# Layer 2's first product by two-by-two blocks: 7 block products in place of 8, cosines on rows of 768 columns, sums of y made on chip

## The chip, the cores and the metric

The program runs on one core of a Trainium2 chip. The metric is the device time of one execution in microseconds (us); lower is better. A core has five engines that run their own instruction streams in order: PE (matmuls; PEld are its weight loads), DVE (vector), ACT (activations), POOL (GpSimd) and SP, which here only issues transfers. Engines wait for each other through semaphores.

## The reference

```python
# attention with random features over 4 sequences of 576 tokens, 8 heads of 64: x is 2304 tokens x 512
phi = lambda x: exp(h - max(h)) / sqrt(m)         # h = x @ omega.T - |x|^2 / 2
x = (phi(q) @ (phi(k).T @ v)) / (phi(q) @ sum(phi(k)) + 1e-6)
# layer 1: 512 -> 1536 -> 512
xn = x / sqrt(mean(x * x) + 1e-6) * rms_g
y = (silu(xn @ w_gate) * (xn @ w_val)) @ w_out
# layer 2: 512 -> 2048 -> 512
h = y @ w_in
out = (h * cos(h)) @ w_out2
```

All is float32. The kernel reaches that accuracy by splitting every operand of a product into a high and a low part of type fp32r and making three products of them (high x high, low x high, high x low), summed in PSUM.

## The kernel before

**Layout.** Activations lie transposed: 128 features on the partitions, tokens along the row. A block is 384 tokens, so 2304 tokens are 6 blocks; two neighbouring blocks are a pair (p = 0, 1, 2). The 512 inputs of a layer are four chunks of 128. A feature block f is 128 columns of the hidden layer: 12 in layer 1, 16 in layer 2.

**Stages.** Attention comes first, with the first four features of layer 1 between its last tiles. Then features 4 to 7 and 8 to 11 of layer 1 run pair by pair, each through `duo` (two features at a time) and `ys` (layer 1's second product). `duo` works on two-by-two blocks: two weight blocks by two halves of the input on one side, two halves of the input by two token blocks on the other, 7 products of combined blocks (names X and Y, by the table `PRODUCTS`) in place of 8; each product is 6 matmuls of 384 columns. Layer 2 follows: for each feature group of `GROUPS2` and each block, one step for each feature: `hidden` makes h in 12 matmuls of 384 columns (4 chunks x 3 parts), ACT and DVE make o = h cos(h) and split it, and `out2` multiplies o by the feature's output weights in 9 matmuls of 512 columns (3 token tiles x 3 parts) into three PSUM banks of sums.

**The cosine.** The chain of one step is: ACT rounds h / 2 pi to an integer (`turns`, L878), DVE subtracts that many turns in two instructions (L879, which reads h in PSUM; L880, which reads two rows in SBUF), ACT takes the sine (L885), DVE multiplies by h (L887, which reads h in PSUM), ACT copies the high part (L888), DVE makes the low part (L890, two rows in SBUF). The step's matmuls of `out2` come two steps after its `hidden`.

**Weights.** The class `Weights` turns the float64 weights into pairs of fp32r, piece by piece (512 columns). A front (DVE L175, L180, L187; ACT L167; POOL L192) makes a float32 piece and keeps it in DRAM. A back reads it again (`b<-kept`) and splits it into a tile of a ring of 20 (ACT L197, POOL L200). For the block products the back also makes sums of pieces (DVE L248, L260, L262, L264). `pace` runs a number of these steps after every unit of the main work, by rates that the main loop sets; `wts.freed` says how many ring tiles are free again.

**Order.** Nothing is scheduled by a program: the order of the code is the order of each engine's queue. `at(d, f)` puts an action off by d units, `unit()` runs what is due.

**Between the layers.** The sums of layer 1's y are completed on DVE (`add_y`, L1118), split (ACT L1070, DVE L1073) and kept in DRAM (`yh_dram`); layer 2 reads blocks of y back (`fetch`, `yhl`). Layer 2's sums over the three feature groups stay in SBUF (`osum`: first group copied, later ones added by `add_up`, L834).

Of the kernel before, what the change touches and what calls it, by code (L numbers as in the profile page):

```python
# [50 lines left out]
FRONT, BACK, BACK_OF_PAIR = 6, 4, 11  # L51
BLOCKED, DONE = "blocked", "done"
# [3 lines left out]
def attention_then_ffn(ctx: ExitStack, tc: tile.TileContext, qT, kT, v, omT, wc1, rms_g, wc2, out, B, H, S, D):  # L56
# [15 lines left out]
    RING, MORE = 20, 2  # L72
# [7 lines left out]
    GROUPS2 = [range(0, 6), range(6, 11), range(11, 16)]  # L80
# [14 lines left out]
    BANKS = {"w": 4, "kv": 2, "q": 2}  # L95
# [3 lines left out]
    def bank(tag, name):  # L99
        return psum.tile([P, 512], F32, tag=tag, name=name, bufs=BANKS[tag])  # L100

# [16 lines left out]
    y_dram = {}  # L118


    class Weights:
# [3 lines left out]
        def __init__(self):  # L125
# [3 lines left out]
            self.todo += [(2, f, e) for f in range(NF2) for e in range(C2)]  # L129
# [10 lines left out]
            self.more = None  # L140
            self.credit = [0.0, 0.0]
            self.first = self.run()
            self.fronts, self.backs = self.all_fronts(), self.all_backs()

        def paired(self, layer, f, e):
            return e if layer == 1 and f not in GROUPS1[0] and e < 2 else None

        def load(self, c, queue=None):
            queue = queue or (nc.scalar if self.early else nc.sync)
            if c < len(self.todo) and c not in self.loaded:  # L150
                self.loaded.add(c)
                layer, f, e = self.todo[c]
# [19 lines left out]
        def front(self, c):  # L172
# [10 lines left out]
            yield  # L183
            self.exponent(c + 1)
# [17 lines left out]
        def split(self, src, key):  # L202
# [5 lines left out]
            if self.paired(layer, f, e) == 0:  # L208
                self.out[1, f, "A11"], self.out[1, f, "A12"] = (t, 0), (t, 256)
# [4 lines left out]
        def ask(self, c):  # L214

            if c in self.kept and c not in self.b:
                b = self.b[c] = conv.tile([P, 512], F32, tag="b", name=f"b{c}", bufs=4)
                nc.sync.dma_start(b, self.kept[c])

        def back(self, c):  # L220
            layer, f, e = self.todo[c]
            whole, one, two = slice(0, 512), slice(0, 256), slice(256, 512)
            while c not in self.kept:
# [32 lines left out]
            self.out[1, f, "S1"], self.out[1, f, "A22"] = (t, 0), (t, 256)  # L256
# [22 lines left out]
            self.out[1, f, "S2"], self.out[1, f, "S3"] = (t, 0), (t, 256)  # L279
            yield  # L280
            self.low(g[:, two], four, at)
            self.out[1, f, "S4"] = (four, 256 * (f % 2))
# [43 lines left out]
        def widen(self, pool):  # L326

            self.more, self.since = pool, self.made

        def buffer(self):  # L330
            c = self.made
            self.made += 1
            more = self.more is not None and (c - self.since) % (RING + MORE) >= RING
            return (self.more if more else wpool).tile([P, 2, 512], F32R, tag="w", name=f"w{c}")

        def room(self):
            wide = self.more is not None and self.made >= self.since + RING
            return self.made < self.freed + RING + (MORE if wide else 0)
# [7 lines left out]
        def pace(self, *rates):  # L346

            for i, rate in enumerate(rates):
# [3 lines left out]
                for _ in range(n):  # L352
                    if next(self.first, DONE) is not DONE:
                        continue
                    if next((self.fronts, self.backs)[i], DONE) in (BLOCKED, DONE):
                        break
                    if i:
                        self.n_back += 1
                    else:
                        self.n_front += 1  # L360
# [159 lines left out]
    with tc.manual_schedule():  # L520
# [59 lines left out]
        def job(n):  # L580
            for _ in range(n):
                if len(combined) < limit[0] and jobs and next(jobs[0], DONE) is DONE:
                    jobs.pop(0)
                    combined.add(len(combined))

        def combinations(p):

            to = t_dram[p] = {n: dram.tile([P, 2, 2, NB], F32, name=f"{n}_dram{p}") for n in ("T1", "T2", "T3", "T4")}
# [25 lines left out]
            for kk in range(2):  # L614
# [31 lines left out]
                lower(s2)  # L646
                keep("T1", kk, s1)
# [20 lines left out]
                lower(s4)  # L668
                keep("T2", kk, s3)
# [4 lines left out]
        def query_step(t, s):  # L674
# [110 lines left out]
        combine = ExitStack()  # L785
# [22 lines left out]
        late = [None]  # L808

        def sum_tile(name):  # L810
            if late[0] is None:
                between.close()
                combine.close()
                late[0] = ctx.enter_context(tc.tile_pool(name="sums", bufs=NBLK, side="right", reuse_waits="tile"))
                wts.widen(ctx.enter_context(tc.tile_pool(name="w2", bufs=MORE, side="right", reuse_waits="tile")))
            return late[0].tile([P, KD * NB], F32, tag="sum", name=name)
# [6 lines left out]
        def put_away(blk, e, ps):  # L823

            y = row(F32, f"y{blk}_{e}") if not more else more[0].tile([P, NB], F32, tag="y", name=f"y{blk}_{e}", bufs=YROWS)
# [6 lines left out]

        def add_up(blk, at, ps):
            nc.vector.tensor_tensor(held[blk][:, at], ps, held[blk][:, at], op=ALU.add)  # L834
# [36 lines left out]
        def hidden(blk, f):  # L871

            w = wts.get(2, f, 0)
            h = bank("w", f"h_ps{blk}_{f}")[:, :NB]
            passes(h, [(two(w, slice(kk * P, (kk + 1) * P)), part(blk, kk)) for kk in range(KD)])
            a, b = row(I32, f"turns{blk}_{f}"), row(F32, f"r{blk}_{f}")

            nc.scalar.activation(a, h, AF.Identity, bias=quarter, scale=1.0 / (2 * math.pi))  # L878
            nc.vector.scalar_tensor_tensor(b, a, -TWO_PI_HI, h, op0=ALU.mult, op1=ALU.add)  # L879
            nc.vector.scalar_tensor_tensor(f32(a), a, -TWO_PI_LO, b, op0=ALU.mult, op1=ALU.add)  # L880
            return h, f32(a)

        def h_cos(blk, f, h, r, front, rate):
            o = fp.tile([P, 2, NB], F32R, tag="t", name=f"o{blk}_{f}", bufs=3)
            nc.scalar.activation(r, r, AF.Sin, bias=half_pi)  # L885
            wts.pace(front / 4, rate / 2)
            nc.vector.tensor_tensor(r, h, r, op=ALU.mult)  # L887
            nc.scalar.copy(o[:, 0], r)  # L888
            wts.pace(front / 4, rate / 2)
            nc.vector.tensor_tensor(o[:, 1], r, f32(o[:, 0]), op=ALU.subtract)  # L890
            return o

        oacc = {}

        def first_sum(blk, j, ps):
            if j == 0:
                held[blk] = sum_tile(f"osum{blk}")
            a = held[blk][:, j * DM:(j + 1) * DM]
            if j % 2:
                nc.vector.tensor_copy(a, ps)  # L900
            else:
                nc.scalar.copy(a, ps)

        def put_out(blk, j):
            t = blk * TPB + j
            nc.sync.dma_start(out[t * P:(t + 1) * P, :], held[blk][:, j * DM:(j + 1) * DM])

        def out2(g, blk, f, o, first, last):
            if first:
# [393 lines left out]
```

## Time and profile before

| | |
|---|---|
| median of 3 runs | 991.6 us (991.59 to 991.62) |
| profiled execution, time | 991.8 us |
| its span in the profile | 990.0 us |
| PE busy | 976.8 us, 99% |
| PEld (weight loads) busy | 923.6 us |
| DVE busy | 674.1 us, 68% |
| ACT busy | 512.1 us, 52% |
| POOL busy | 361.7 us, 37% |
| moved by DMA | 194.58 MB, mean 197 GB/s |
| mean granted clock of PE | 0.996 |

The profile is one execution; its time is its span and 1.8 us around it, and lies 0.2 us above the median. PE has something in flight in 99% of the span, so what is left to read is how fast its matmuls follow each other and where the few idle microseconds are. Matmuls overlap: the pace is the distance between starts, not the duration of one.

### The profile page before, as it was taken

Reading aid. Unit: us, or ns where it says so; the run is one execution under the profiler, and the core shown is the slowest. Engines: PE = TensorE matmul, PEld = TensorE weight load, DVE = VectorE, ACT = ScalarE, POOL = GpSimd, SP = SyncE. Lnnn points to the kernel's source line nnn. Section 1 sums busy time; section 2 is a strip of 40 time slices with the busy share of each in tenths; the row PEclk is TensorE's granted clock in tenths of the full one; section 3 lists DMA queues with packets and bytes.
Section 4 is the critical chain, followed back from the end, with each engine's and each line's share of the span. In section 5 each row is a group of like instructions: output and inputs, shape, how many; then the busy total and the mean of one; then the engine's idle time right before and its main releaser. Section 6 shows DMA issues by size and latency. Waiting matters only on the chain.

```text
span 990.0 us, 16129 instructions
## 1 busy us (share of the span) xinstructions
PE 976.8 (99%) x5905; PEld 923.6 (93%) x5905; DVE 674.1 (68%) x1195; ACT 512.1 (52%) x1117; POOL 361.7 (37%) x333
## 2 busy tenths in 40 slices
PE   9999999998999999999999989999999999999998
PEld 8988999998999999999999988999999999999997
DVE  5786778788854466686665767666667776666565
ACT  7787776675434442536443545554444544344433
POOL 2133348647926865476441742211112310000000
PEclk9999999999999999999999999999999999999999
DMA  8555268876696989657988875433224432014201
GB/s 303 159 170 181 83 227 285 269 286 223 247 326 237 364 291 346 222 164 276 356 291 302 323 253 193 125 131 129 64 107 161 161 143 78 1 37 154 98 32 64
DMA packets 81438, 194.58 MB, mean 197 GB/s; under 512 B 8016, under 2 KB 38864, under 8 KB 81360
## 3 DMA queue, kind: packets, MB, share of 16 engines
q1 hardware_dynamic: 79920, 188.78, 54.8%
q10 hardware_dynamic: 1440, 4.78, 1.4%
q8 instruction: 46, 0.75, 0.3%
q14 instruction: 32, 0.26, 0.1%
HBM read 136.38 MB, written 57.15 MB: 195 GB/s over the span
## 4 chain that ended last, share of the span: by engine, by line
PE 89%; DVE 4%; POOL 2%; DMA 2%; issue 2%; ACT 2%; SPq 0%; ACTq 0%; DVEq 0%; POOLq 0%
PE h_ps L798 20%; PE X L1062 10%; PE y L1141 10%; PE Y L1062 8%; PE gv_ps L798 7%; PE o_ps L792 7%; PE o_ps L791 7%; PE o_ps L790 7%; PE y_ps L863 4%; PE kv_ps L562 4%; PE num_ps L439 2%; PE kp_ps L401 2%; PE qp_ps L401 2%; PE eT_ps L419 1%; DMA x_dram<-xhl 1%
## 5 line engine op out<-in xcount | busy, mean ns | idle before, releaser
L798 PE MATMUL h_ps<-yhl,w 128*128 128x384 f32 x1152 | 217.5, 337 | 0.0
L798 PEld LDWEIGHTS h_ps<-yhl,w 128*128 128x128 f32 x1152 | 205.2, 188 | 8.2
L192 POOL TENSOR_TENSOR f<-f,raw 128x512 f32<-128x512 f32 x68 | 93.9, 1381 | 286.1 <-DVE raw L187 251.9
L200 POOL TENSOR_TENSOR w<-b,w 128x512 fp32r<-128x512 f32 x72 | 95.2, 1327 | 80.6 <-ACT w L197 71.3
L885 ACT ACTIVATE turns<-turns,half_pi 128x384 f32<-128x384 f32 x96 | 59.2, 617 | 109.9 <-DVE turns L880 109.9
L790 PE MATMUL o_ps<-w,o 128*128 128x512 f32 x288 | 112.5, 391 | 2.6 <-ACT o L888 2.6
L792 PE MATMUL o_ps<-w,o 128*128 128x512 f32 x288 | 114.6, 398 | 0.0
L791 PE MATMUL o_ps<-w,o 128*128 128x512 f32 x288 | 114.2, 396 | 0.0
L798 PE MATMUL gv_ps<-xhl,w 128*128 128x384 f32 x576 | 108.3, 336 | 1.1 <-DVE eT L429 0.4
L798 PEld LDWEIGHTS gv_ps<-xhl,w 128*128 128x128 f32 x576 | 100.7, 188 | 2.2 <-DVE eT L429 0.7
L1141 PE MATMUL y<-t,w 128*128 128x384 f32 x576 | 101.0, 334 | 0.0
L1141 PEld LDWEIGHTS y<-t,w 128*128 128x128 f32 x576 | 99.9, 188 | 0.0
L890 DVE TENSOR_TENSOR o<-turns,o 128x384 fp32r<-128x384 f32 x96 | 55.9, 583 | 51.8 <-ACT o L888 51.2
L887 DVE TENSOR_TENSOR turns<-h_ps,turns 128x384 f32<-128x384 f32 x96 | 53.4, 556 | 44.2 <-ACT turns L885 43.4
L888 ACT CAST o<-turns 128x384 fp32r<-128x384 f32 x96 | 49.3, 513 | 65.9 <-DVE turns L887 65.3
L1062 PE MATMUL X<-T,w 128*128 128x384 f32 x432 | 80.7, 334 | 0.0
L879 DVE SCALAR_TENSOR_TENSOR r<-turns,h_ps 128x384 f32<-128x384 int32 x96 | 53.1, 553 | 39.0 <-ACT turns L878 38.9
L1062 PEld LDWEIGHTS X<-T,w 128*128 128x128 f32 x432 | 75.4, 188 | 0.0
L878 ACT ACTIVATE turns<-h_ps,quarter 128x384 int32<-128x384 f32 x96 | 55.5, 579 | 35.2 <-PE h_ps L798 34.9
L792 PEld LDWEIGHTS o_ps<-w,o 128*128 128x128 f32 x288 | 54.3, 189 | 11.9 <-DVE o L890 0.3
L790 PEld LDWEIGHTS o_ps<-w,o 128*128 128x128 f32 x288 | 54.2, 188 | 11.6 <-ACT o L888 3.0
L880 DVE SCALAR_TENSOR_TENSOR turns<-turns,r 128x384 f32<-128x384 int32 x96 | 61.6, 641 | 3.3
(98 smaller groups left out, 1714.5 us busy)
## 6 DMA issues: line engine op xcount, KB each, us to landing
raw<-wc SPq DMA_DIRECT2D x59, 512.0 KB, 5.1
yhl<-yh_dram SPq DMA_DIRECT2D x32, 768.0 KB, 5.7
T<-T_dram SPq DMA_DIRECT2D x20, 768.0 KB, 9.1
kept<-f SPq DMA_DIRECT2D x56, 256.0 KB, 5.3
b<-kept SPq DMA_DIRECT2D x56, 256.0 KB, 4.6
B<-x_dram SPq DMA_DIRECT2D x15, 768.0 KB, 6.6
x_dram<-xhl SPq DMA_DIRECT2D x12, 768.0 KB, 5.8
s<-x_dram SPq DMA_DIRECT2D x24, 384.0 KB, 5.9
```

Source lines behind the costliest of these rows:

```text
L192: nc.gpsimd.tensor_tensor(f32(f), f32(f), rest, op=ALU.add)
L200: nc.gpsimd.tensor_tensor(t[:, 1, to], src, f32(t[:, 0, to]), op=ALU.subtract)
L790: nc.tensor.matmul(o, w[0], x[0], start=first, stop=False)
L791: nc.tensor.matmul(o, w[0], x[1], start=False, stop=False)
L792: nc.tensor.matmul(o, w[1], x[0], start=False, stop=last)
L798: nc.tensor.matmul(o, w[i], x[j], start=n == 0, stop=n == len(terms) - 1)
L878: nc.scalar.activation(a, h, AF.Identity, bias=quarter, scale=1.0 / (2 * math.pi))
L880: nc.vector.scalar_tensor_tensor(f32(a), a, -TWO_PI_LO, b, op0=ALU.mult, op1=ALU.add)
L885: nc.scalar.activation(r, r, AF.Sin, bias=half_pi)
L890: nc.vector.tensor_tensor(o[:, 1], r, f32(o[:, 0]), op=ALU.subtract)
L1062: nc.tensor.matmul(o, w[:, i, c + kk * P:c + (kk + 1) * P], x[:, j, kk], start=begin and n == 0, stop=n == 5, skip_group_check=True)
L1141: nc.tensor.matmul(acc[e], w[:, i, e * P:(e + 1) * P], t[:, j], start=f == fs[0] and i + j == 0, stop=f == fs[-1] and j == 1)
```

## The change

Layer 2's first product now works like layer 1's `duo`. A period is one pair of features (f, f + 1) by one pair of blocks, 24 periods in all; its `hidden(k, i)` is one of 7 products of 6 matmuls, and the 36 matmuls of `out2` of the period before stand in runs of 5 or so between them. Layer 1's last `ys` carries the first period's 7 products between its matmuls. The groups of feature pairs are {0, 1, 2}, {3, 4, 5}, {6, 7}; within a group the pairs of blocks take turns.

The results of the products are copied (ACT) or added (DVE) from PSUM into rows of SBUF, two chains (feature by block) side by side, and `cosine` treats them as one row of 768 columns. The high and low parts are still made for each chain (384 columns). The combinations of y that the products need (T1 to T4) are made on POOL (`mix`), ACT and DVE while y is still in SBUF. The sums of layer 2 are no longer held in SBUF over the groups: a run of periods on one pair of blocks leaves its six sums in DRAM, and the next run adds them (`evict`, `ask_sum`); seven runs evict 42 tiles of 256 KB, of which 24 go to DRAM and come back. At the end of a run the seven inputs of the next (768 KB each) are loaded during one period. The weights of layer 2 need the sums of pieces too: seven half tiles for a feature where there were four. Fronts and backs are kept apart from their loads by `LAG_OF_RAW` and `LAG_OF_KEPT` units.

```diff
-    GROUPS2 = [range(0, 6), range(6, 11), range(11, 16)]
+    GROUPS2 = [[0, 1, 2], [3, 4, 5], [6, 7]]
+    PARTS2 = [6, 5, 6]
...
+            while self.too_new(self.loaded_at, c + 1, LAG_OF_RAW):
+                yield BLOCKED
...
+            while self.too_new(self.asked_at, c, LAG_OF_KEPT):
+                yield BLOCKED
...
+        def mix(p, name, kk):
+            a, b, c, d = (whole[2 * p + side, 2 * i + kk] for side, i in ((0, 0), (1, 0), (1, 1), (0, 1)))
+            o, x, y = {"T1": (a, b, a), "T3": (b, c, b), "T2": (c, c, a), "T4": (d, d, c)}[name]
+            nc.gpsimd.tensor_tensor(o, x, y, op=ALU.subtract)
+            at(2, mix_high, p, name, kk, o)
...
+        def hidden(k, i):
...
+            o = banks2[k, acc]
+            seventh(o, 2, p, f, which, name, i in (0, 1, 3))
+            if i in (0, 2, 3, 6):
+                if i in (2, 6) or (k, i) == (0, 0):
+                    rows2[k + (i > 2), i // 2 % 3] = two_rows(F32, f"h{i}_{k}")
+                a = rows2[k, 1][:, 3 - i] if i in (2, 3) else rows2[k + (i > 2), 0][:, int(i == 0)]
+                nc.scalar.copy(a, o)
+            else:
+                a = rows2[k, int(i > 1)][:, (1, 0, 1)[(1, 4, 5).index(i)]]
+                nc.vector.tensor_tensor(a, o, a, op=ALU.add)
+            if i == 1:
+                cosine(k, rows2.pop((k, 0)), ([(k - 1, 2 * periods[k - 1][3] + 1, 2 * periods[k - 1][2])] if k else [])
+                       + [(k, f, 2 * p)])
...
+            elif i == 5:
+                cosine(k, rows2.pop((k, 1)), [(k, f + 1, 2 * p + 1), (k, f, 2 * p + 1)])
...
+            def reduce():
+                nc.vector.scalar_tensor_tensor(b, a, -TWO_PI_HI, h, op0=ALU.mult, op1=ALU.add)
+                nc.vector.scalar_tensor_tensor(r, a, -TWO_PI_LO, b, op0=ALU.mult, op1=ALU.add)
+
+            def cut(i):
+                o = turned[of[i]] = halves("o%d_%d_%d" % of[i])
+                split(o, r[:, i])
+                at(int(of[i][0] + 1 < NPER), lower, o, r[:, i], nc.vector)
+
+            at(1, nc.scalar.activation, a, h, AF.Identity, quarter, 1.0 / (2 * math.pi))
+            at(2, reduce)
+            at(3, nc.scalar.activation, r, r, AF.Sin, half_pi)
+            at(4, lambda: nc.vector.tensor_tensor(r, h, r, op=ALU.mult))
+            for i in range(len(of)):
+                at(5 + i, cut, i)
...
+            share = [0, 3, 6, 6, 7, 7, 7] if begins_run[k] or k + 1 == NPER else [5, 5, 5, 5, 5, 5, 6]
+            for i in range(7):
+                hidden(k, i)
+                unit()
+                for _ in range(share[i]):
+                    next(o)
+                unit()
```

**DVE, in the middle of layer 2.** Before, a step in the first group of features (feature 7 on block 0; `h_ps` is h in PSUM, `turns` and `r` are rows in SBUF, `o` the split result):

```order
L879 SCALAR_TENSOR_TENSOR r0_7_8511<-turns0_7_8510,h_ps0_7_8497 128x384
L880 SCALAR_TENSOR_TENSOR turns0_7_8510<-turns0_7_8510,r0_7_8511 128x384
L887 TENSOR_TENSOR turns0_7_8510<-h_ps0_7_8497,turns0_7_8510 128x384
L890 TENSOR_TENSOR o0_7_8534<-turns0_7_8510,o0_7_8534 128x384
```

Now, DVE in period 8 (pair of blocks 0, third pair of features; `h6`, `h2` are rows of h in SBUF, `Yh`, `Xh` the products in PSUM, `f57`, `raw57`, `b53` pieces of weights):

```order
L1187 TENSOR_TENSOR h6_7_8066<-Yh_8_8083,h6_7_8066 128x384
L1049 TENSOR_TENSOR o7_3_1_8097<-turns7_3_1_7_2_1_8048,o7_3_1_8097 128x384
L190 TENSOR_SCALAR f57_8112<-W57_8077 128x512
L1049 TENSOR_TENSOR o7_2_1_8109<-turns7_3_1_7_2_1_8048,o7_2_1_8109 128x384
L274 TENSOR_TENSOR b53_8039<-b53_8039 128x256
L1208 SCALAR_TENSOR_TENSOR r7_3_0_8_4_0_8108<-turns7_3_0_8_4_0_8107,h6_7_8066 128x768
L1209 SCALAR_TENSOR_TENSOR turns7_3_0_8_4_0_8107<-turns7_3_0_8_4_0_8107,r7_3_0_8_4_0_8108 128x768
L195 TENSOR_SCALAR raw57_7985<-f57_8112 128x512
L1219 TENSOR_TENSOR turns7_3_0_8_4_0_8107<-h6_7_8066,turns7_3_0_8_4_0_8107 128x768
L204 SCALAR_TENSOR_TENSOR raw57_7985<-raw57_7985 128x512
L287 TENSOR_TENSOR b53_8039<-b53_8039,b52_8026 128x256
L289 TENSOR_TENSOR b53_8039<-b53_8039 128x256
```

What moved: the two instructions that read h in PSUM (L879, L887) became L1208 and L1219, which read it in SBUF and are twice as long, and instructions on weights stand between them.

**POOL, periods 7 and 8 now.** `f` rows are fronts, `w` rows backs (low parts of ring tiles):

```order
L217 TENSOR_TENSOR w68_7928<-b48_7115,w68_7928 128x256
L209 TENSOR_TENSOR f54_7855<-f54_7855,raw54_7594 128x512
L209 TENSOR_TENSOR f55_7962<-f55_7962,raw55_7803 128x512
L217 TENSOR_TENSOR w69_8024<-b50_7932,w69_8024 128x512
L217 TENSOR_TENSOR w70_8037<-b51_7934,w70_8037 128x512
L209 TENSOR_TENSOR f56_8035<-f56_8035,raw56_7882 128x512
L217 TENSOR_TENSOR w71_8114<-b52_8026,w71_8114 128x512
L217 TENSOR_TENSOR w72_8140<-b53_8039,w72_8140 128x512
L209 TENSOR_TENSOR f57_8112<-f57_8112,raw57_7985 128x512
L217 TENSOR_TENSOR w73_8183<-b53_8039,w73_8183 128x512
L217 TENSOR_TENSOR w68_7928<-b52_8026,w68_7928 128x256
L217 TENSOR_TENSOR w74_8207<-b54_8116,w74_8207 128x512
```

What moved: 12 instructions stand within two periods here, 5 in period 7 and 7 in period 8; in the layer 2 of before there are 36 over all its 96 steps.

## Rows read from the trace of the kernel before

**Rows 1.** The page's first part: busy us (share of the span) x instructions.

```profile
PE 976.8 (99%) x5905; PEld 923.6 (93%) x5905; DVE 674.1 (68%) x1195; ACT 512.1 (52%) x1117; POOL 361.7 (37%) x333
```

**Rows 2.** Timeline of PE, layer 2: start, duration (us), instruction, [idle before].

```profile
592.98 0.50 PE L790 MATMUL o_ps<-w,o 128*128 128x512 f32 x1 [2.65 <-ACT o L888]
...
596.52 2.59 PE L798 MATMUL h_ps<-yhl,w 128*128 128x384 f32 x12
598.95 0.39 PE L790 MATMUL o_ps<-w,o 128*128 128x512 f32 x1
...
601.03 2.27 PE L798 MATMUL h_ps<-yhl,w 128*128 128x384 f32 x12
603.14 0.39 PE L790 MATMUL o_ps<-w,o 128*128 128x512 f32 x1
...
605.22 2.27 PE L798 MATMUL h_ps<-yhl,w 128*128 128x384 f32 x12
```

**Rows 3.** Timeline of PE: the last run of 27 `out2` matmuls, first and last.

```profile
979.91 0.39 PE L790 MATMUL o_ps<-w,o 128*128 128x512 f32 x1
...
985.81 0.39 PE L792 MATMUL o_ps<-w,o 128*128 128x512 f32 x1
```

**Rows 4.** Stages: us, busy of PE, PEld, DVE, ACT, POOL, granted clock, DMA share, GB/s.

```profile
266.00:305.00 39.00, 39.00 (x228) 38.96 (x227) 21.06 (x38) 13.03 (x29) 15.70 (x15) 1.00 0.94 340
443.00:575.00 132.00, 132.00 (x763) 132.00 (x762) 88.52 (x142) 64.38 (x132) 66.00 (x55) 1.00 0.85 308
590.00:600.00 10.00, 7.35 (x28) 5.89 (x28) 7.33 (x14) 4.53 (x9) 1.44 (x2) 0.83 0.79 260
600.00:700.00 100.00, 100.00 (x504) 90.66 (x503) 67.26 (x122) 51.74 (x94) 17.28 (x13) 1.00 0.39 130
```

**Rows 5.** Timeline of DVE just before the PE wait of Rows 2.

```profile
587.47 2.12 DVE L1073 TENSOR_TENSOR yhl<-y,yhl 128x384 fp32r<-128x384 f32 x3
589.51 0.54 DVE L879 SCALAR_TENSOR_TENSOR r<-turns,h_ps 128x384 f32<-128x384 int32 x1
590.09 1.06 DVE L880 SCALAR_TENSOR_TENSOR turns<-turns,r 128x384 f32<-128x384 int32 x1
```

**Rows 6.** The tile `turns`: ns min/median/max of each instruction on it.

```profile
L878 ACT ACTIVATE turns<-h_ps,quarter x96: 567/580/584, 579.9 to 978.1; 128x384 int32<-128x384 f32 x96
L879 DVE SCALAR_TENSOR_TENSOR r<-turns,h_ps x96: 540/554/557, 580.6 to 978.7; 128x384 f32<-128x384 int32 x96
L880 DVE SCALAR_TENSOR_TENSOR turns<-turns,r x96: 557/558/1673, 581.1 to 979.3; 128x384 f32<-128x384 int32 x96
L885 ACT ACTIVATE turns<-turns,half_pi x96: 598/617/622, 581.7 to 980.8; 128x384 f32<-128x384 f32 x96
L887 DVE TENSOR_TENSOR turns<-h_ps,turns x96: 542/558/559, 582.4 to 981.4; 128x384 f32<-128x384 f32 x96
```

**Rows 7.** Groups of DVE in 443 to 575 us: busy us, mean ns | idle before.

```profile
L1073 DVE TENSOR_TENSOR t<-r,t 128x384 fp32r<-128x384 f32 x12 | 13.4, 1128 | 1.1 <-ACT t L1070 1.1
L187 DVE SCALAR_TENSOR_TENSOR raw<-raw 128x512 f32<-128x512 uint32 x12 | 11.8, 987 | 0.1
L1073 DVE TENSOR_TENSOR yhl<-y,yhl 128x384 fp32r<-128x384 f32 x18 | 10.7, 609 | 3.9 <-ACT yhl L1070 3.8
L180 DVE TENSOR_SCALAR raw<-f 128x512 int32<-128x512 int32 x12 | 9.5, 793 | 0.0
L175 DVE TENSOR_SCALAR f<-W 128x512 int32<-128x512 int32 x12 | 7.7, 641 | 0.0
```

**Rows 8.** Groups of DVE in 600 to 700 us.

```profile
L187 DVE SCALAR_TENSOR_TENSOR raw<-raw 128x512 f32<-128x512 uint32 x7 | 4.8, 684 | 0.0
L175 DVE TENSOR_SCALAR f<-W 128x512 int32<-128x512 int32 x7 | 2.9, 418 | 0.0
```

**Rows 9.** One group of DVE over the whole span.

```profile
L834 DVE TENSOR_TENSOR osum<-o_ps,osum 128x512 f32<-128x512 f32 x36 | 23.1, 682 | 1.7 <-PE o_ps L792 1.7
```

**Rows 10.** Timeline of POOL, one back with nothing beside it.

```profile
801.28 1.28 POOL L200 TENSOR_TENSOR w<-b,w 128x512 fp32r<-128x512 f32 x1 [7.06 <-ACT w L197]
```

More of the change, by code (lines that the diff above doesn't have):

```diff
@@ L351, in pace @@
                 self.credit[i] -= n
[L352 to L360, printed above, removed]
+                while n:
+                    if next(self.first, DONE) is DONE:
+                        if next((self.fronts, self.backs)[i], DONE) in (BLOCKED, DONE):
+                            if self.now:
+                                self.credit[i] += min(n, 2)
+                            break
+                        if i:
+                            self.n_back += 1
+                        else:
+                            self.n_front += 1
+                    n -= 1
         def get(self, layer, f, e):
@@ L868, in out1 @@
                 waits.append((put_away, blk, e, yacc[blk][e]))
[L871 to L909, printed above, removed]
-                oacc[blk] = [bank_of_sums(f"o_ps{g}_{blk}_{f}_{j}") for j in range(TPB)]
-            w = wts.get(2, f, 1)
-            for j in range(TPB):
-                mm3(oacc[blk][j], two(o, slice(j * P, (j + 1) * P)), two(w), first, last)
-            if not last:
-                return
-            for j in range(TPB):
-                if g == 0:
-                    waits.append((first_sum, blk, j, oacc[blk][j]))
-                else:
-                    waits.append((add_up, blk, slice(j * DM, (j + 1) * DM), oacc[blk][j]))
-                if g == len(GROUPS2) - 1:
-                    waits.append((put_out, blk, j))
         def steps_of(groups, orders):
@@ L1042, in unit @@
         def unit():
[L1043 removed]
+            now = due.setdefault(clock[0], [])
+            while now:
+                f, args = now.pop(0)
                 f(*args)
+            del due[clock[0]]
             flush(1)
[L1046 removed]
+            wts.now += 1
+            wts.pace(*tempo)
             job(2 if clock[0] % 5 < 2 else 1)
@@ new lines, in out2 @@
+        def out2(k):
+            n, g, p, fq = periods[k]
+            f, a, b = 2 * fq, 2 * p, 2 * p + 1
+            for slot, (ff, blk) in enumerate([(f, a), (f + 1, b), (f, b), (f + 1, a)]):
+                first, last = begins_run[k] and slot < 2, ends_run[k] and slot > 1
+                if first:
+                    oacc[blk] = [bank(t, f"o_ps{k}_{blk}_{j}") for j, t in enumerate(
+                        ["wb", "wb", "kv"] if blk == a else ["kv", "q", "q"])]
+                o, w = turned.pop((k, ff, blk)), wts.get(2, ff, 1)
+                for j in range(TPB):
+                    js = slice(j * P, (j + 1) * P)
+                    for n, (x, y) in enumerate(((0, 0), (0, 1), (1, 0))):
+                        nc.tensor.matmul(oacc[blk][j], o[:, x, js], w[:, y], start=first and n == 0,
+                                         stop=last and n == 2)
+                        if last and n == 2:
+                            at(0, evict, k, blk, j, oacc[blk][j])
+                        yield
```

365 lines of the change are left out of this document (220 added, 145 removed).

## The prediction

> **What bounds the kernel now.** I read the page's first part, then the timeline of PE in layer 2, then stages by windows, then what POOL does to DVE. First: PE has something in flight in 99% of the span, DVE in 68%, ACT in 52%, POOL in 37% [rows 1]. So the time is the pace of the matmuls plus the few places where PE waits, and a matmul taken away counts in full as long as the others still keep up. Second: in layer 2 a step runs from 601.03 to 605.22, 4.19 us: its 12 matmuls of h take 2.11 and its 9 of o 2.08, with no idle time between them [rows 2]. There is one true wait, 2.65 us before 592.98, for ACT's o. DVE shows why [rows 5]: three low parts of y stand in its queue ahead of the first cosine's L879, and L880 then takes 1.06. Third, the stages [rows 4]: the mean step of layer 2 uses DVE for 67 of 100 us and POOL for 17. The middle of layer 1 uses DVE 88.5 and POOL 66 of 132 us, and PE there never stops.
>
> **Term 1, matmuls.** Before, the 96 steps have 96 x 12 = 1152 matmuls for h; now 24 periods have 42 each, 1008. So 144 matmuls of 384 columns go; the 864 of o stay. At 2.11 / 12 = 0.176 us [rows 2] that is 25.3 us. But the order of the two kinds changes. In a step the 9 o take 2.08, 0.231 each; in an unmixed run of 27 the pace is (985.81 - 979.91) / 26 = 0.2269 [rows 3], 2.04 for 9. A round trip between the kinds therefore costs at least 0.04 on the o side alone. Four steps had 4 round trips and a period has 7, so 72 more in all: 2.9 us, and with as much again on the side of h 5.8. Bounds: 20 saved, or 25 (29, if splitting the runs costs nothing and o even falls to 0.227: 864 x 0.004 = 3.5 more). I take the middle between 20 and 25: **-23**.
>
> **Term 2, the wait at the start of layer 2.** It costs 2.65 us idle, then 9 o that take 3.54 instead of 2.08, then 12 h that take 2.43 instead of 2.11 [rows 2], while the granted clock of 590 to 600 is 0.83 [rows 4], so part of this stretch was at 1.2 and not 2.4 GHz, after the idle time. 2.65 + 1.46 + 0.32 = **-4.4** if it goes. Now the first 7 products lie between layer 1's last matmuls, so h is there earlier; what the handover costs instead is priced with the new waits.
>
> **Term 3, new waits of DVE.** What does DVE have in a period? Three additions of a product in PSUM (0.555 each, as L879 and L887 [rows 6]); two chains of three instructions of 768 columns; four low parts of 384 (0.558 [rows 6]). No row has 768 columns. From 384 columns (0.558) to 512 (0.682 [rows 9]) the price grows by 0.124, so 768 is an estimated 0.558 + 3 x 0.124 = 0.93. Sum 1.67 + 5.58 + 2.23 = 9.5 us, against a period of PE of 42 x 0.176 + 36 x 0.231 = 15.7. Alone that fits. The work on weights is on top, and POOL gets in the way:
>
> The two instructions on `turns` that read h in PSUM never take more than 0.557 and 0.559 in 96 times; L880, with two rows in SBUF, has the same median and a maximum of 1.673 [rows 6]. The excess of 1.1 is a little less than one POOL instruction, 1.28 [rows 10]. So DVE instructions with both operands in SBUF can stand behind a POOL instruction, and those with an operand in PSUM don't. The change moves L879 and L887 to the first kind (L1208, L1219).
>
> How much per instruction? In 443 to 575 us the five exposed groups [rows 7] exceed their bare price (0.558 for 384 columns [rows 6], 0.684 for L187 [rows 8], 0.418 for the tensor-scalar lines L175 and L180 [rows 8]) by 12 x 0.57 + 18 x 0.05 + 12 x 0.30 + 12 x 0.375 + 12 x 0.22 = 18.5 us over 66 instructions, 0.28 each, with POOL busy half the time. Per exposed instruction that is 0.56 us x the share of POOL.
>
> A period whose DVE sum is D, with n exposed instructions and P us of POOL, then needs T = D + 0.56 n P / T. For period 8: D = 9.5 + 4 tensor-scalars of 0.418 + one of 0.684 + 4 of 256 columns (0.43 by the same slope) = 13.6; n = 6 + 4 + 9 = 19; P = 6 x 1.28 + one half-wide of some 0.9 = 8.6. T = 18.5, 2.8 over the 15.7. The same with the instructions in each period of the change's order:
>
> - period 1 (layer 1's last y, mixing T2 to T4, backs): D 15.1, n 17, P 11.6, T 20.5, +4.7
> - periods 2, 6: +0.5, +0.3
> - period 7: D 14.6, n 17, P 6.0, +2.0
> - period 8: +2.8; period 10: D 13.5, n 19, P 7.3, +2.1
> - period 13: D 16.4, n 22, P 5.2, +3.9
> - all others: T below the period, 0.
>
> Sum 16. Two things make it smaller: a DVE instruction can start 0.08 before the end of the one before it (587.47 + 2.12 against 589.51 [rows 5]), and a low part is needed only some time after it is made, a slack of about 1 us for each of three stretches. Bounds: 0, as the middle of layer 1 hides all such waits [rows 4]; and 41, the sum of D + P - 15.7 over the hot periods, if DVE and POOL never overlap. I take **+10**, nearer to the lower end, because the measured excess is a quarter of what full exclusion would give. PE's waits of over 2 us are likely in one or two places (period 1, where y's additions and low parts stand ahead of the first o as they did before; period 8 or 13); one of them will cost clock again, 1.46 + 0.32 = 1.8 [rows 2]: **+2** (0 to 5).
>
> The Trainium skill, "SBUF — State Buffer", section "Who interferes with whom", speaks against the change: DVE and GpSimd share one pair of ports as an exclusive lock, a DVE instruction with two SBUF inputs contends with a GpSimd instruction that reads SBUF, and the loser blocks for the whole instruction. This trace agrees on which instructions vary, and shows 0.28 each and not a whole 1.28; by the rule taken at its harshest the last case below would come.
>
> **Costed at nothing.** Attention and the first features of layer 1: each engine's order is unchanged there. The copies of products: ACT has at most 19 instructions in a period, four of 768 columns (at most 2 x 0.617 [rows 6]) and 15 of at most 0.62, 14.2 of 15.7, and ACT's `turns` rows don't vary [rows 6]. Evictions: 42 tiles for 48, same width. Spilled sums: 24 tiles out and back, 12.6 MB spread over layer 2, where DMA is 39% busy [rows 4]. Loads at a change of run: 7 x 768 KB = 5.5 MB in 15.7 us is 350 GB/s; the trace has reached 340 [rows 4]. The last is needed most of a period after the first, so nothing is late unless the rate falls under some 200 GB/s; then each of six changes could lose up to 2 us, 12 in all. The end (about 4 us after the last matmul) is the same.
>
> **Sum.** The profiled execution takes 991.8 (span 990.0 and 1.8 around it), 0.2 over the median, so from 991.6: - 23 - 4.4 + 10 + 2 = **976**.
>
> **Rivals.**
> - *No new waits.* DVE and POOL overlap as in the middle of layer 1, where DVE at 67% with POOL at 50% cost PE nothing [rows 4]. 991.6 - 23 - 4.4 = 964. Against it: there the exposed DVE work is smaller, and period 1 is over its time even without POOL's part (15.1 of 15.7). Chance 0.20.
> - *DVE becomes the bound through the weight periods.* POOL's excess per instruction grows with the longer rows (0.93 instead of 0.56 lies open to POOL for longer), waits of 22 to 30 us, and more of them long enough to lose the clock (+2 to 5): 985 to 995. Chance 0.17.
> - *Slower: full exclusion.* If each exposed DVE instruction and each POOL instruction run one after the other, the hot periods lose 41 us: 991.6 - 27.4 + 41 = 1005. It decides against the change from 27.4 lost on. For it: the maximum of L880 is nearly a whole POOL instruction [rows 6]. Against: the mean in 443 to 575 us [rows 7]. This is the Trainium skill's rule named above, without any overlap. Chance 0.08.
> - *Loads late at the changes of run*, together with the +10: 988 to 995. Chance 0.03.
> - That the change doesn't remove what it says is excluded: the order has 144 matmuls fewer.
>
> My forecast, 968 to 983, has 0.52. What a measurement can tell from no change is 0.2%, 2 us. Faster by more: 0.52 + 0.20 + somewhat over half of the second rival, 0.82; within 2 us: 0.07; slower: 0.08 and a few hundredths, 0.11. The range 962 to 990 leaves out the lower tail of the first rival and what ends above.
>
> **What would show it.** Term 1: 42 + 36 matmuls in 15.7 to 16.0 us in a period without weights, say 14 to 18. Term 2: no wait of 2.6 us at the first o; instead some idle time within period 1, behind DVE. Term 3: L1187, with PSUM, never above 0.56; L1208, L1209, L1219 with a median near 0.93 and maxima up to 1.3 higher; PE idle in periods 1, 7 to 10 and 13 and hardly elsewhere, released by ACT's o or DVE's low part. I am wrong if those periods show no idle time (first rival), if PE waits in periods with no weights (then the chain itself or the loads are too slow), or if the pace of matmuls within a period is above 0.206 us on average with PE never idle (term 1).

## The result and the profile after

The changed kernel takes 1001.2 us (median of 4; 1000.5 to 1001.6) against 991.6: 1.0097 times as long, 95% interval 1.0079 to 1.0114. The forecast was 976, the range 962 to 990. The profiled execution has a span of 999.9 us.

The page's first part, to be held against [rows 1]: PE has 144 matmuls fewer and 12 us less busy, in a span that is 10 us longer.

```profile
PE 964.7 (96%) x5761; PEld 902.6 (90%) x5761; DVE 728.6 (73%) x1173; ACT 536.3 (54%) x1149; POOL 414.6 (41%) x373
```

PE's idle time by what ended it (in all, times, longest; us). Before, the first line of this view had 2.6 us and everything else lay ahead of the pairs of layer 1.

```profile
PE o_ps L1236 <- ACT o L1046: 11.6, 7, 3.5
PE X L1038 <- ACT r L1066: 5.7, 2, 3.1
...
PE Y L1038 <- DVE r L1069: 1.8, 2, 1.5
PE y L1138 <- POOL w L217: 1.8, 3, 0.9
PE o_ps L1236 <- DVE o L1263: 1.5, 1, 1.5
```

The lines with X, Y and y are layer 1, a stage that the prediction put at nothing. A ledger by stages, from the starts of matmuls in the timeline of PE; "least" is the same work without any wait. A unit of layer 1 is here the 168 matmuls of block products of four features on one pair of blocks, from its first matmul to its last:

| stage, us | before | least | after |
|---|---|---|---|
| first pair of layer 1 begins at | 303.1 | | 301.3 |
| from there to the last block product of layer 1 | 257.9 | 257.9 | 273.5 |
| of it: the units of features 8 to 11 on their second and third pair of blocks | 28.95, 28.95 | 28.95, 28.95 | 35.75, 33.93 |
| from there to the last matmul | 424.8 | | 421.1 |
| of it: periods 1 and 2 | | 31.4 | 40.5 |
| periods 7 to 11 | | 78.5 | 91.0 |
| periods 12 to 18 | | 109.9 | 114.4 |

**Layer 2.** Twelve of the periods (3 to 6, 10, 12, 15, 16, 19 to 22) take 15.65 to 15.75 us with no idle time, so the saving itself is there: 24 x 15.7 = 377 for the 96 x 4.19 = 402 of before, -25.4. The wait at the first o of layer 2 is gone too. Then 26 us of stalls come back. The longest wait stands in period 2, which takes 21.9 us:

```profile
627.12 0.80 PE L1236 MATMUL o_ps<-w,o 128*128 128x512 f32 x1 [3.45 <-ACT o L1046]
```

How a stall comes about is read from period 8, on PE (start, duration, [idle before]), then DVE, then POOL:

```profile
721.78 1.32 PE L1038 MATMUL Xh<-B,w 128*128 128x384 f32 x6
722.95 1.32 PE L1236 MATMUL o_ps<-w,o 128*128 128x512 f32 x5
724.11 1.23 PE L1038 MATMUL Yh<-B,w 128*128 128x384 f32 x6
725.17 1.08 PE L1236 MATMUL o_ps<-w,o 128*128 128x512 f32 x4
728.19 0.79 PE L1236 MATMUL o_ps<-w,o 128*128 128x512 f32 x1 [1.93 <-ACT o L1046]
```

```profile
716.78 3.05 DVE L1049 TENSOR_TENSOR o<-turns,o 128x384 fp32r<-128x384 f32 x2
719.75 1.51 DVE L190 TENSOR_SCALAR f<-W 128x512 int32<-128x512 int32 x1
721.18 0.55 DVE L1187 TENSOR_TENSOR h<-Yh,h 128x384 f32<-128x384 f32 x1
...
725.75 1.84 DVE L1219 TENSOR_TENSOR turns<-h,turns 128x768 f32<-128x768 f32 x1 [0.40 <-ACT turns L1012]
```

```profile
716.53 1.31 POOL L209 TENSOR_TENSOR f<-f,raw 128x512 f32<-128x512 f32 x1 [5.79 <-DMA b<-kept]
717.80 3.18 POOL L217 TENSOR_TENSOR w<-b,w 128x512 fp32r<-128x512 f32 x2
...
725.49 1.29 POOL L209 TENSOR_TENSOR f<-f,raw 128x512 f32<-128x512 f32 x1 [4.50 <-PE Yh L1038]
```

Two low parts take 3.05 instead of 1.1 and L190 1.51 instead of 0.42, while POOL has three instructions one behind the other; so h (L1187) comes late, and L1219 then takes 1.84 instead of 0.96 beside POOL's next. About 3.9 us are lost in one chain; what its slack does not take is the 1.93 that PE stands still. Over layer 2, ns min/median/max:

```profile
L1049 DVE TENSOR_TENSOR o<-turns,o x96: 541/551/1648, 597.3 to 991.9; 128x384 fp32r<-128x384 f32 x96
L1208 DVE SCALAR_TENSOR_TENSOR r<-turns,h x50: 545/957/2054, 593.1 to 988.9; 128x768 f32<-128x768 int32 x46, 128x384 f32<-128x384 int32 x4
L1187 DVE TENSOR_TENSOR h<-Xh,h x24: 546/558/558, 596.9 to 981.2; 128x384 f32<-128x384 f32 x24
```

As foreseen: the instruction with an operand in PSUM never varies, those with both operands in SBUF do; 768 columns take 0.957 (estimate 0.93).

**Layer 1.** PE and ACT in the first of the two long units:

```profile
519.19 1.63 PE L1038 MATMUL X<-T,w 128*128 128x384 f32 x6 [3.11 <-ACT r L1066]
```

```profile
509.35 0.52 ACT L1119 CAST T3h<-y 128x384 fp32r<-128x384 f32 x1
513.01 0.51 ACT L1119 CAST T2h<-y 128x384 fp32r<-128x384 f32 x1 [3.14 <-DMA T_dram<-y]
513.43 0.52 ACT L1043 ACTIVATE r<-r 128x384 f32<-128x384 f32 x1
513.86 0.46 ACT L1066 COPY r<-X 128x384 f32<-128x384 f32 x1
517.84 0.51 ACT L1119 CAST T4h<-y 128x384 fp32r<-128x384 f32 x1 [3.52 <-DMA T_dram<-T3h]
518.26 0.52 ACT L1043 ACTIVATE r<-r 128x384 f32<-128x384 f32 x1
518.68 0.46 ACT L1066 COPY r<-X 128x384 f32<-128x384 f32 x1
```

L1119 is the copy of the high part of T (`mix_high`). It needs a row of the ring of 13 that y, T and their transfers to DRAM share, and waits until a transfer has freed one; behind it stand L1066, which empties a product's PSUM bank, and so PE (3.1 us).

**The clock** after such waits (columns as in [rows 4]): 5 us at a mean of 0.66 are 3.4 us at 1.2 GHz.

```profile
519.00:524.00 5.00, 4.81 (x19) 4.81 (x20) 1.67 (x3) 1.43 (x4) 0.02 (x1) 0.66 0.92 289
570.00:575.00 5.00, 5.00 (x20) 5.00 (x21) 1.72 (x4) 2.19 (x5) 1.90 (x2) 0.66 0.90 266
625.00:633.00 8.00, 5.88 (x17) 5.33 (x18) 6.45 (x9) 5.00 (x9) 4.76 (x4) 0.57 0.87 290
727.00:732.00 5.00, 3.81 (x11) 3.48 (x12) 4.86 (x8) 3.28 (x6) 1.52 (x1) 0.66 0.69 210
748.00:752.00 4.00, 3.84 (x12) 3.41 (x13) 3.56 (x7) 2.88 (x6) 0.45 (x1) 0.59 0.72 247
```

### The profile page after: what moved, and what is told of

Read it like the earlier page. It is cut to its first block, busy times and chain, and to the rows that moved or that the text cites. A ratio compares the mean times of both kernels' runs of the same rounds, so it can differ in the third digit from the quotient of the medians.

```text
span 999.9 us, 16241 instructions
## 1 busy us (share of the span) xinstructions
PE 964.7 (96%) x5761; PEld 902.6 (90%) x5761; DVE 728.6 (73%) x1173; ACT 536.3 (54%) x1149; POOL 414.6 (41%) x373
## 5 line engine op out<-in xcount | busy, mean ns | idle before, releaser
L1236 PE MATMUL o_ps<-w,o 128*128 128x512 f32 x864 | 230.8, 399 | 14.8 <-ACT o L1046 11.6
L1236 PEld LDWEIGHTS o_ps<-w,o 128*128 128x128 f32 x864 | 161.6, 190 | 45.2 <-ACT o L1046 15.2
L209 POOL TENSOR_TENSOR f<-f,raw 128x512 f32<-128x512 f32 x68 | 94.9, 1395 | 221.9 <-DVE raw L204 181.0
L217 POOL TENSOR_TENSOR w<-b,w 128x512 fp32r<-128x512 f32 x88 | 116.5, 1331 | 169.7 <-ACT w L214 154.3
L1038 PE MATMUL Xh<-T,w 128*128 128x384 f32 x432 | 90.3, 345 | 0.0
L1038 PEld LDWEIGHTS Xh<-T,w 128*128 128x128 f32 x432 | 80.4, 193 | 5.5
L1219 DVE TENSOR_TENSOR turns<-h,turns 128x768 f32<-128x768 f32 (+1 forms) x50 | 51.3, 1026 | 32.0 <-ACT turns L1012 31.8
L214 ACT CAST w<-b 128x512 fp32r<-128x512 f32 x88 | 50.3, 582 | 31.2 <-DVE b L274 25.6
L1049 DVE TENSOR_TENSOR o<-turns,o 128x384 fp32r<-128x384 f32 x96 | 65.5, 713 | 1.6 <-ACT o L1046 1.0
L884 PE MATMUL y_ps<-t,w 128*128 128x384 f32 x288 | 61.5, 349 | 0.0
L1208 DVE SCALAR_TENSOR_TENSOR r<-turns,h 128x768 f32<-128x768 int32 (+1 forms) x50 | 48.3, 965 | 15.8 <-ACT turns L1012 15.0
L1038 PE MATMUL Yh<-B,w 128*128 128x384 f32 x288 | 58.7, 338 | 0.4 <-ACT h L1184 0.4
L204 DVE SCALAR_TENSOR_TENSOR raw<-raw 128x512 f32<-128x512 uint32 x68 | 56.5, 831 | 0.5
```

Source lines behind the costliest of these rows:

```text
L204: nc.vector.scalar_tensor_tensor(rest, raw[:, :, 0].bitcast(U32), 2.0 ** -52, rest, op0=ALU.mult, op1=ALU.mult)
L209: nc.gpsimd.tensor_tensor(f32(f), f32(f), rest, op=ALU.add)
L217: nc.gpsimd.tensor_tensor(t[:, 1, to], src, f32(t[:, 0, to]), op=ALU.subtract)
L884: nc.tensor.matmul(yacc[blk][e], w[:, i, e * P:(e + 1) * P], t[:, j], start=first and i + j == 0, stop=last and j == 1)
L1038: nc.tensor.matmul(o, w[:, i, c + kk * P:c + (kk + 1) * P], x[:, j, kk], start=begin and n == 0, stop=n == 5, skip_group_check=True)
L1049: engine.tensor_tensor(t[:, 1], a, f32(t[:, 0]), op=ALU.subtract)
```

## The experiments

Theory of the prediction, kept at first: POOL's instructions hold up DVE's that have both operands in SBUF (**lock**), and DVE and POOL together need more than a period (**balance**). Against it: the chain of one cosine is too long for its slack (**chain**); the DVE instructions on weights ahead of it are the delay, with or without POOL (**queue**). For layer 1: **rows** (a copy on ACT waits for a row that a transfer still holds, with the emptying of PSUM behind it) against DVE and POOL being over their time.

**e1, later slots of o**

```diff
-            share = [0, 3, 6, 6, 7, 7, 7] if begins_run[k] or k + 1 == NPER else [5, 5, 5, 5, 5, 5, 6]
+            share = [0, 3, 6, 6, 7, 7, 7]
```

> Only the order of PE in layer 2 changes: in every period the matmuls of o start later (0, 3, 6, 6, 7, 7, 7 behind the seven products instead of 5, 5, 5, 5, 5, 5, 6), so that the second slot of o starts after four products of h and not after two. Theory chain (the stalls are the latency of one cosine chain against its slack): the slack grows by two products less some o, about 2.1 us, the stalls of 1.9 us in periods 8, 9 and 11 and the smaller ones of 7, 13, 14, 17 and 18 go, and layer 2 loses some 5 us instead of 26; about 980 us. Theory throughput (the prediction's: DVE and POOL together need more than 15.7 us in a hot period): the same time is needed wherever o stands, at most a few us come back, 995 to 999 us. Layer 1 keeps its 15.6 us in both.

999.1 us, ratio 1.0068 (1.0044 to 1.0093), an interval that overlaps the one of the change. All but 0.4 us of the waits for o is gone, and others stand in their place:

```profile
PE Xh L1038 <- ACT h L1184: 11.9, 9, 2.9
...
PE Yh L1038 <- ACT h L1184: 2.7, 4, 1.1
```

ACT's copy of a product now waits in its queue behind the sine, which waits for DVE. Periods 14 and 17 lose nothing any more (15.65 us each; 16.9 and 16.3 in the change), as chain has it, but periods 7 to 11 take 92.2 us (91.0): more slack at one place is no remedy where DVE itself is late. The total lies at the upper end of what balance forecast. DVE is not full in every period that stalls, though: it is busy 18.6 of 20.6 us in period 8 and 16.0 of 19.9 in period 11, so balance alone does not account for the second.

**e2, e7, mix spread in layer 1**

```diff
-                    at(6 + 3 * m // 2 if p else ...
+                    at(6 + 2 * m if p else ...                                          # e2
+                    at(6 + 2 * m if p == 2 else 4 + 7 * m // 4 if p == 1 else ...       # e7
```

> Only the making of T1 to T4 of y (mix) in layer 1 is spread: one every two units of work instead of one every one and a half. Theory row reuse: the two stalls of layer 1 (3.1 and 2.6 us, each with a fall of the clock behind it) come from ACT's copy of T2 and T4, which waits until a transfer to DRAM has freed its row, with the copy of a product behind it; with more time between the copies the wait shrinks and 8 to 11 us come back, 991 to 993 us. Rival theory: DVE and POOL are simply over their time there with the extra work of mix, then the spread moves the stalls and gives back under 3 us, 998 to 1001 us.

998.3 us (1.0041 to 1.0083). The two units fall to 30.1 and 30.3 us, 9.2 in all, but a new wait of 4.0 us stands at the handover: the rows for y of the last pair come late (PE for DVE's L1099), and period 0 takes 19.4 us instead of 13.5. So the total is the one that the rival forecast, while the two units did what rows says.

> The mix of the first pair of blocks one every two units, that of the second one every 1.75 units but begun two units earlier. Theory row reuse: the earlier run's new wait at the handover (4.0 us, DVE's addition of y behind a row that a late mix still held) goes, and the gain of layer 1 stays: 8 to 10 us less than the change as it is, 991 to 993 us. If the 13 rows are short whatever the order, the wait comes back in one of the two places: 996 to 999 us.

994.2 us (1.0015 to 1.0044): units of 32.6 and 30.9, period 0 13.5 again. Some 7 us come back, less than the 8 to 10 expected.

**e3, POOL writes zeros and reads nothing**

```diff
         def low(self, src, t, to):
-            nc.gpsimd.tensor_tensor(t[:, 1, to], src, f32(t[:, 0, to]), op=ALU.subtract)
+            nc.gpsimd.memset(f32(t[:, 1, to]), 0.0)    # from period 4 on; L209 likewise
```

> From period 4 on POOL's instructions on weights are replaced by ones that write zeros of the same size and read nothing (so the low parts and the sums of these weights are left out). DVE's and ACT's queues are unchanged. Theory lock: DVE's instructions with two operands in SBUF no longer wait for POOL, the low parts of o and L1219 go back to 0.55 and 0.96 us without outliers, and the stalls of periods 7 to 13 go: 13 to 15 us less, about 987 us. Rival theory queue: the chain is late because of the DVE instructions on weights that stand ahead of it; they are still there, and under 4 us come back, 997 to 1001 us.

987.1 us, a single run, which leaves out the low parts of the weights from period 4 on. Every period from 7 to 18 takes 15.65 to 15.75 but one (13, 16.7). DVE's queue is the same, its durations are not (e3, 705 to 830 us; its lines stand 7 further down, L1056 is L1049 of the change):

```profile
L1056 DVE TENSOR_TENSOR o<-turns,o x32: 546/550/553, 709.1 to 827.3; 128x384 fp32r<-128x384 f32 x32
L1216 DVE SCALAR_TENSOR_TENSOR turns<-turns,r x16: 957/957/960, 704.1 to 822.3; 128x768 f32<-128x768 int32 x16
L1226 DVE TENSOR_TENSOR turns<-h,turns x16: 948/958/960, 706.1 to 824.2; 128x768 f32<-128x768 f32 x16
```

Not one outlier in 64 (L1049, L1209, L1219 of the change reach 1.65 to 1.95 in the same stretch). So the delay comes from POOL, and not from the queue. That it comes from POOL's reading is less firmly shown, because a write of zeros is also shorter (0.53 us, where L209 and L217 take 1.3 to 1.5), and POOL is busy 2.7 us in period 8 instead of 9.6: with the 15 of L1208 counted in, only ten of these DVE instructions ran beside a POOL instruction, for up to 0.53 us, and none of the ten was late. In the change 14 of the 22 that ran beside POOL were late.

**e4, e1 and e2 together**

> The first two together. If they act on separate stages, their gains add up: by the theories chain and row reuse 970 to 973 us, faster than the kernel before by 2%; by throughput and the rival of the second 990 to 999 us.

996.0 us (1.0029 to 1.0059): both gains small, and their sum (2.1 and 2.9) is what the two together bring.

**e5, fronts out of periods 9 to 11**

```diff
-            tempo[:] = 0.0 if loading or k < 4 else wts.rate(len(wts.todo) + 1, 14 * (14 - k)), ...
+            tempo[:] = wts.rate(FRONTS_UPTO[k], 14) if k in FRONTS_UPTO else 0.0, ...
+        FRONTS_UPTO = {3: 53, 4: 56, 6: 58, 7: 60, 12: 62, 13: 64, 15: 67, 16: 69}
```

> Only the times of the weights' fronts (DVE and POOL) in layer 2 change: the nine that group 1 needs stand in periods 3, 4, 6 and 7 and the eight of group 2 in 12, 13, 15 and 16, so that periods 9 to 11 hold none. Theory of the balance of DVE and POOL (T = D + 0.56 n P / T): period 9 then has D 10.5 and four POOL instructions, T under 15.7, and the stalls of 9 and 11 (6.2 us in all with their clock) and most of period 8's 4.2 go; periods 3 and 4 with two fronts each stay under; 991 to 995 us. Rival: the stalls belong to the backs (ring tiles made just in time) and not to the balance, then 9 and 11 keep theirs; 999 to 1002 us.

1012.9 us. The part that was asked came true: 9 and 11 take 15.75, 10 takes 16.2. Period 8 was to lose most of its stall too and keeps it (19.6 us, 20.0 in the change). A back also needs its piece and the next one kept, so the last back of group 1 lacked a front until period 12 (29.2 us, PE for ACT's w, 8.9 in all); that was my schedule's mistake. And period 4 with its fronts takes 18.4, 16 takes 18.7: what leaves one period stalls another.

**e6, the last pair's mix two periods later**

```diff
-... else 6 + (0, 2, 3, 6)[m % 4] + 14 * kk, mix, p, name, kk)
+... else 28 + (0, 2, 3, 6)[m % 4] + 14 * kk, mix, p, name, kk)
```

> Only the mix of the last pair of blocks (8 POOL, 8 ACT, 8 DVE instructions) moves from periods 1 and 2 to 3 and 4, where POOL has nothing to do. Theory balance: period 1 has D 13.4 and P 7.3 and period 2 loses nearly all its exposed extra, the 3.5 us stall of period 2 with its clock (6.2 us) goes and period 1's 2.9 us become 1 or so; 992 to 995 us. Rival: the stalls of periods 1 and 2 come from y's last additions and low parts and from the backs, which stay; 998 to 1001 us.

998.3 us (1.0048 to 1.0097). Periods 1 and 2 take 34.2 instead of 40.5, as expected; 3 takes 1.6 more, and 8 and 11 together 2.1 more, so that the total stays in the range of the rival, whose mechanism the periods rule out.

**e8, e5, e6 and e7 together**

> All three moves: mix by pair, mix of the last pair later, fronts out of periods 8 to 11 (group 1's in 4 to 7). If the lock of DVE and POOL and the rows are the whole loss, the gains add up: 1001 - 8 - 7 - 8 = about 978 us, faster than the kernel before. If work only moves its stalls along, 988 to 995 us.

1006.9 us: the missing front of e5 again (period 12: 29.9); without its 14 us it would be about 993 (an estimate), the rival's value. To move work along is not enough here; what is left to try is less DVE work that is open to the lock.

**e9 to e12, one instruction less in the chain**

```diff
-                nc.vector.scalar_tensor_tensor(b, a, -TWO_PI_HI, h, op0=ALU.mult, op1=ALU.add)
-                nc.vector.scalar_tensor_tensor(r, a, -TWO_PI_LO, b, op0=ALU.mult, op1=ALU.add)
+                nc.vector.scalar_tensor_tensor(r, a, -2.0 * math.pi, h, op0=ALU.mult, op1=ALU.add)
```

h is at most 4.6 in size on these inputs and the number of turns 0 or 1, so one subtraction of 2 pi in float32 is enough here. e10 adds e6 and e7, e11 e1 as well; e12 has the edit in the kernel before.

> The change with one instruction for the reduction by turns of 2 pi (one product by 2 pi) in place of two, L1209 is gone and with it one row: each chain has 0.96 us less of DVE work that is open to the lock. Theory balance and lock: period 8 has D 11.7, n 17, P 8.6, T about 16.6 instead of 18.5, all others fall under 15.7 but 1 and 13; of layer 2's 26 us of stalls 12 to 18 come back, 983 to 989 us. Rival: the chain is only one instruction shorter and POOL's bursts stall it as before: 3 to 6 us, 995 to 998 us. Layer 1 keeps its 15.6 us in both.

> The same with the two moves of mix (spread by pair in layer 1, the last pair's in periods 3 and 4). If the stages add up: 986 - 6 to 8 in layer 1 - 3 to 5 in periods 1 to 4 = 973 to 978 us, faster than the kernel before by over 1%. By the rival 984 to 989 us.

> The run before with the later slots of o as well. With shorter chains DVE is no longer over its time in most periods, so that now a later slot can take up what is left: 968 to 975 us. If ACT's copies of h are still late behind the sine, the stalls move to the products as they did with the longer chain: no gain over the run before, 973 to 980 us.

> The kernel before with one reduction in place of two. PE sets its time and waits only at the start of layer 2, where L880 with its 1.06 us stands in the chain that is waited for: 0 to 2 us less, 990 to 991.6 us. It shows what the edit is worth without the change.

| run | us | ratio to before (95%) | periods 1 and 2 | 7 to 11 | 12 to 18 |
|---|---|---|---|---|---|
| change | 1001.2 | 1.0097 (1.0079 to 1.0114) | 40.5 | 91.0 | 114.4 |
| e9 | 981.7 | 0.9902 (0.9882 to 0.9922) | 36.6 | 81.1 | 110.0 |
| e10 | 971.4 | 0.9796 (0.9780 to 0.9812) | 32.1 | 81.1 | 110.0 |
| e11 | 969.4 | 0.9779 (0.9764 to 0.9793) | 32.1 | 80.3 | 109.5 |
| e12 | 988.7 | 0.9972 (0.9961 to 0.9983) | | | |

One DVE instruction less per chain brings 19.5 us in the change, 18.2 of them in the three groups of periods of the table, and 2.7 in the kernel before, where PE is the bound. The waits for o in e9 are (11.6, 7 and 3.5 in the change):

```profile
PE o_ps L1234 <- ACT o L1046: 3.4, 2, 2.4
```

The edit takes work off DVE, shortens the chain by the same 0.96 us and frees a row, so by itself it does not tell balance from chain; e1, which gave the chain about 2 us of slack and brought little, speaks for the work. e9, e10 and e12 came out 1 to 2 us below their forecasts. The 2 us between e10 and e11 are not shown to be slack: in 13 periods that had no stall in e10 either, a period takes 15.65 us instead of 15.75, because `out2` stands in six runs instead of seven (1.3 us in all; e1 has the same pace), and 0.5 us come from periods 8 and 9. e11 is faster than both kernels; over 704 to 796 us PE is busy 91.0 of 92 us, where the change has 84.7:

```profile
704.00:796.00 92.00, 91.00 (x449) 80.54 (x448) 77.91 (x113) 55.39 (x98) 35.01 (x25) 1.00 0.54 177
```

**e13 to e15, rows and ACT's queue in layer 1**

```diff
-        OWN, EXTRA = 3, 5             # e13, e15: two more rows, one tile of t and o less
-        YOWN, YROWS, YMORE = 4, 3, 6
+        OWN, EXTRA = 3, 4
+        YOWN, YROWS, YMORE = 4, 3, 8
-            nc.scalar.copy(h.bitcast(F32R), o)          # e14
+            nc.gpsimd.tensor_copy(h.bitcast(F32R), o)
```

> The change with 15 rows for y and T in place of 13 (paid with one of the eight tiles for t and o), mix in its old spacing. Theory row reuse: the two units of layer 1 in which T is made (35.8 and 33.9 us against 28.9 without mix) fall to 29 to 31, 6 to 10 us less in all, 991 to 995 us. Rival, DVE and POOL over their time by mix: both stay over 33 us, 999 to 1002 us.

> The change with the 24 copies of the high part of T on POOL in place of ACT, so that a wait for a row stands in POOL's queue and not ahead of ACT's copies of products. Theory in-order ACT: the waits of PE for ACT's L1066 (5.7 us) go, at the price of 24 more POOL instructions under the lock; layer 1's two units fall to 30 to 33 us, 994 to 999 us. Rival, DVE and POOL over their time: more POOL work makes both units longer, 1002 to 1008 us.

> One reduction, later slots, the last pair's mix later, and 15 rows with the old spacing of mix in layer 1. By row reuse the two units of layer 1 come near 29 to 30 us (30.3 and 31.2 in the version with spread mix) and the total to 964 to 968 us; if seven tiles for t and o are too few, stalls in layer 2 take it back to 970 to 975 us.

e13: 1003.1 us, above both of its forecasts. The units with mix fall to 30.8 and 30.2 at the old spacing, as rows would have it, but an earlier unit, features 4 to 7 on the third pair, grows from 29.4 to 36.1, where combinations come late from DRAM:

```profile
PE X L1038 <- DMA T<-T_dram: 4.5, 1, 4.5
```

e14: 996.9 us (1.0037 to 1.0077), units of 30.4 and 30.7, no wait for L1066. e15: 977.8 us, also above both, with e13's wait (4.6 us). Why the wider ring or the smaller one of tiles makes that load late was not followed up.

## Why the prediction was wrong, step by step

| term of the sum | predicted | measured |
|---|---|---|
| 1, matmuls | -23 | -25.4 |
| 2, wait at the start of layer 2 | -4.4 | -4.4, no such wait is left |
| 3, new waits of DVE in layer 2, with the clock | +10, +2 | +26.2 (idle 15.1) |
| costed at nothing: attention | 0 | -1.9, same order; not explained |
| layer 1, in no list | 0 | +15.6 |
| sum from 991.8 | 976 | 1001.9 (profiled 999.9 + 1.8) |

**Terms 1 and 2** held. The pace in a period is 15.7 us, as worked out; the part of the saving that was set aside for round trips was not needed.

**The step that failed most is the list of what costs nothing.** The change has `mix`, 24 times a POOL, an ACT and a DVE instruction and two transfers, and 16 of them run under layer 1's products. The prediction priced only the eight that fall in periods 1 and 2, and left the 16 at nothing, without a reason, in a stage where PE had never stopped [rows 4]. Two units lost 11.8 of the 15.6 us there. e2, e13 and e14 take the wait away in three ways (time between, more rows, another queue) and each brings both units to 30 to 31 us: the cause is a copy that waits for a row in ACT's queue, ahead of the emptying of PSUM. The 1 to 2 us by which each stays above 28.95 are not explained. Of the other 3.8 us, the profile shows 1.8 as waits for POOL's w; no run was made on them.

**Term 3 had the mechanism right and the size wrong.** Price per exposed instruction: in 600 to 860 us of the change the groups of L1049, L1208, L1209, L1219, L190, L195 and L204 exceed their bare durations by 27.6 us over 203 instructions, 0.14 each at a POOL share of 74.4 / 260 = 0.29, which is 0.48 us x the share (predicted 0.56). The three that lose most (busy us, mean ns; bare 0.55, 0.96 and 0.96 us each):

```profile
L1049 DVE TENSOR_TENSOR o<-turns,o 128x384 fp32r<-128x384 f32 x60 | 43.3, 748 | 0.9 <-ACT o L1046 0.4
L1209 DVE SCALAR_TENSOR_TENSOR turns<-turns,r 128x768 f32<-128x768 int32 x31 | 34.7, 1121 | 1.1
L1219 DVE TENSOR_TENSOR turns<-h,turns 128x768 f32<-128x768 f32 x30 | 33.4, 1113 | 16.6 <-ACT turns L1012 16.4
```

The table of periods summed to 16, and PE's idle time in layer 2 is 15.1. That the two agree is in part luck: period 2, at 0.5 in the table, loses 6.2 (5.5 of it with the mixing of the last pair, as e6 shows), periods 9 and 11, at 0, lose 3.9 and 2.3, and period 10, at 2.1, loses nothing. Two things were wrong around it. First, the 16 were cut to 10 for slack between periods: no such saving shows, as a delay falls on one chain and PE stands at once. Second, what a wait costs beyond its idle time was put at 2 us: it is 26.2 - 15.1 = 11. Of these up to 6.8 are the clock: 6.9, 3.4 and 3.3 us at 1.2 GHz, in the last three windows above, at half the pace. Some 2 more are the restart: in period 8 the distance between the two o around the wait is 2.32, where pace and idle time make 2.16, and there are 13 such waits (an estimate, 13 x 0.16). The last 2 or so were not taken apart.

**The rivals.** The total came out near the one that had a chance of 0.08, but not by its mechanism: full exclusion in layer 2 would have lost 41 us there, and 26 were lost. Layer 2 by itself would have given 991.6 - 25.4 - 4.4 + 26.2 = 988, within the rival in which DVE becomes the bound (985 to 995), but not for its reason: the excess did not grow with the longer rows (0.20 us each for L1049 with 384 columns, 0.16 for L1209 and L1219 with 768). What carried the total over the line was layer 1. Loads at the changes of run cost nothing that shows: no wait of PE in layer 2 is put down to a DMA. The Trainium skill, "SBUF — State Buffer", section "Who interferes with whom", says that a DVE instruction with two SBUF inputs contends with a GpSimd instruction that reads SBUF and not with one that only writes it. e3 agrees as far as it goes: with POOL writing alone, none of 64 instructions is late, though few of them ran beside POOL.

## What to carry to other kernels

Count a change's new instructions in every stage in which they run, with each buffer they need and each transfer that frees it: a copy that waits for a buffer stops all that stands behind it on its engine. Where PE is to be made faster, price a wait at its idle time and as much again where the clock falls (1.93 us idle in periods 8 and 9, 4.3 and 3.9 lost), and give a sum of small delays no credit for slack that no row shows. If the engine that becomes short is one that another engine can hold up, take instructions off it before moving them about: one of 0.96 us per chain brought 19.5 us here, and of the rearrangements the best brought 7.

## What the hardware showed that was not expected

- The clock fell after waits of PE of 3.1, 2.6, 3.5, 1.93 and 1.93 us (the five windows), and not after a third one of 1.93 us before 783.38: the window 782 to 788 us has a granted clock of 1.00. In e12 the wait at the start of layer 2 is 1.16 us in place of 2.65, and the clock does not fall behind it (1.00 over 590 to 600 us, 0.83 in the kernel before).
- A tensor-scalar instruction (L190, one operand in SBUF) takes 0.42 alone and 1.51 beside POOL in period 8: it is open to the lock as those with two operands are. The prediction's rule named only the latter, though its price counted both.
